# Splitting the logits of every second attention step around half a value tile

## The chip, the cores and the metric

The kernel runs on one core of one Trainium2 chip. The core has five engines with an instruction queue each: TensorE (matmuls, called PE in the profile), VectorE (DVE), ScalarE (ACT), GpSimd (POOL) and SyncE (SP, which here only issues DMAs). Each queue is worked through in order, and the engines wait for one another on semaphores. The metric is the time of one execution on the device in microseconds (us): before the change 1191.71 us, the median of 5 runs from 1191.21 to 1194.92.

## The reference, cut to what matters

Four layers run one after the other on a residual stream x of 2048 positions by 576 features: attention, gated MLP, attention, gated MLP.

```python
x = x + _A_ref(_layernorm(x), A_wqkv, A_wo)
x = x + _B_ref(_layernorm(x), B_w_in, B_w_sp, B_b_sp, B_w_out)
x = x + _A_ref(_layernorm(x), A_wqkv, A_wo)
x = x + _B_ref(_layernorm(x), B_w_in, B_w_sp, B_b_sp, B_w_out)
```

The attention has 32 heads of 18 features. Position s attends to 8 positions, s, s-2, ..., s-14, those below 0 masked:

```python
idx = pos[:, None] - off[None, :]          # off = 0, 2, ..., 14
logits = einsum('bhsd,bhswd->bhsw', q, kg) * scale
attn = softmax(where(mask, logits, -1e9))
o = einsum('bhsw,bhswd->bhsd', attn, vg)   # then o @ wo
```

The MLP multiplies gelu(x @ w_in[:, :half]) by a gate, which mixes the normalized other half over all positions with a 2048 by 2048 matrix, and projects back with w_out.

## The kernel before, in words

An attention layer (`layer_A`) cuts the 2048 queries into 19 tiles of 112 (the last has 32), each with its 16 preceding keys, so that a tile's keys are 128 rows. The window is not gathered: q and k carry extra rows that make the logit of every key outside the window very small, so full 128 by 112 logit blocks can be computed and exponentiated. 

Each tile is worked in two steps of 16 heads, 38 steps `s` in all (`NST`). A step uses these pieces, named as in the code:

- `L_mm(s)` (line 428): 16 matmuls of 32 by 128 weights and 112 columns into two PSUM tiles `L_ps`, `jp` = 0 and 1, 8 matmuls each. Heads lie in groups of 32 rows, and a matmul uses only the 32-row strip `32*j` of the array (`tile_position`). Half `jp` = 0 uses strips 0 and 1, half `jp` = 1 strips 2 and 3. Both tiles come from the tag `H`, which has two slots, so each half of step s+1 writes the slot that the same half of step s used, and waits until that has been read.
- `EXP(s)` (line 442): two ScalarE activations, one for each half, from `L_ps` to `P_sb` in SBUF. There are four `P_sb` buffers, two steps' worth.
- `PV(s)` (line 449): 16 matmuls of the full array, 19 columns each (18 features and the row of ones that gives the softmax sum), into `O_ps`, then on VectorE a reciprocal and a product into `o_t`. After the second step of a tile, SP issues a transposing DMA from `o_t` to the ring buffer `oT`.
- `VW(t, hh, dve)` (line 375): half a v tile: 5 matmuls of the full array, 288 columns each, into a PSUM tile `pv`, then one cast to `v_ext`, on VectorE if `dve`, else on ScalarE. In the stretch of the change the half `hh` = 0 lies at even steps and is cast on VectorE, the half `hh` = 1 lies at odd steps and is cast on ScalarE.
- `WO(i, hh)` (line 487): half an output tile of 128 positions: 5 matmuls of 288 columns from `oT` into `pw`, then the residual sum on VectorE. `LN_STATS`, `LN_XN` (on GpSimd), `XST` and `LN_T` (a store and a transposing DMA on SP) follow for each tile.

`pv`, `O_ps`, `pw`, `pp` and `pt` share the PSUM tag `PT`, which has four slots handed out in program order.

All of this is in a manual schedule: each engine's queue holds its instructions in the order in which the Python code emits them. The loop at line 707 sets the order around the change. In step s it emits `L_mm(s + 1)`, `EXP(s + 1)`, `PV(s)`, and then what the dictionary `table` holds for s: the projections `PG` of the second half of q and k (up to step `PG_END` = 14), then `VW`, then the output pieces. So the logits run one step ahead of the product with v, and a v tile is made some steps before it is used: `VW(t, 0)` stands at step 2t-2, `VW(t, 1)` at 2t-1, and `PV` needs them at step 2t. The tile t = 9 of the first attention is an exception, made at steps 0 and 13, and in the first attention the v tiles up to 8 are made ahead of the loop.

From step 14 on, a usual step on TensorE is thus `L_mm(s + 1)`, `PV(s)`, one `VW` half, one `WO` half. Steps 22 and 23 of the first attention have no `WO`, nor have steps 21 and 22 of the second. Steps 25 and 32 of the first and 32 of the second have two.

Of the kernel before, what the change touches and what calls it, by code (L numbers as in the profile page):

```python
# [62 lines left out]
class K:  # L63
# [258 lines left out]
    def layer_A(self, li):  # L322
# [32 lines left out]
        def tdim(t):  # L355
            nq = min(QT, S - QT * t)
            return HALO + nq, nq
# [11 lines left out]
        def evac(out, in_, dve):  # L369
            if dve:  # L370
                nc.vector.tensor_copy(out=out, in_=in_)  # L371
            else:
                nc.scalar.copy(out=out, in_=in_)

        def VW(t, hh, dve):
            nk = tdim(t)[0]
            pv = self.PT_tile([P, 512], f32, "pv")
            for c in range(5):
                nc.tensor.matmul(pv[:nk, 0:288], lhsT=self.xnT[:, c, QT * t:QT * t + nk],  # L379
                                 rhs=wv_sb[:, c, hh * 288:(hh + 1) * 288], start=(c == 0), stop=(c == 4))  # L380
            evac(v_ext[:nk, t, 16 * hh:16 * hh + 16, 0:DH], pv[:nk, 0:288].rearrange("p (b d) -> p b d", d=DH), dve)
# [43 lines left out]
        NST = 2 * NT  # L425
        L_tiles = {}

        def L_mm(s):
            t, hf = divmod(s, 2)
            nk, nq = tdim(t)  # L430
            L_tiles[s] = [self.H_tile("L_ps") for _ in range(2)]
            for jp in range(2):
                for ftl in range(4):
                    g = 4 * hf + ftl
                    for jj in range(2):
                        j = 2 * jp + jj
                        nc.tensor.matmul(L_tiles[s][jp][:nk, jj, ftl * QT:ftl * QT + nq],  # L437
                                         lhsT=kT[32 * j:32 * j + 32, g, QT * t:QT * t + nk],
                                         rhs=qT[32 * j:32 * j + 32, g, QT * t + PADL:QT * t + PADL + nq],
                                         start=True, stop=True, tile_position=(32 * j, 0))  # L440

        def EXP(s):
            nk, nq = tdim(s // 2)
            for jp, L_ps in enumerate(L_tiles.pop(s)):
                Lv = L_ps[:, :, 0:4 * QT].rearrange("p a (b c) -> p a b c", c=QT)
                nc.scalar.activation(out=P_bufs[(2 * s + jp) % 4][:nk, :, :, 0:nq], in_=Lv[:nk, :, :, 0:nq], func=ACT.Exp,  # L446
                                     scale=scale)

        def PV(s):
            t, hf = divmod(s, 2)  # L450
            nk, nq = tdim(t)
            O_ps = self.PT_tile([P, 512], f32, "O_ps")
            for jp in range(2):
                for ftl in range(4):
                    for jj in range(2):
                        idx = 4 * ftl + 2 * jp + jj
                        nc.tensor.matmul(O_ps[:, idx * (DH + 1):(idx + 1) * (DH + 1)],  # L457
                                         lhsT=P_bufs[(2 * s + jp) % 4][:nk, jj, ftl, :],
                                         rhs=v_ext[:nk, t, 16 * hf + idx, :], start=True, stop=True)
            Ov = O_ps[:, 0:16 * (DH + 1)].rearrange("p (h e) -> p h e", e=DH + 1)  # L460
            o_t = o_bufs[t % len(o_bufs)]
            rec = sb.tile([P, 16], f32, name="rec", tag="rec", bufs=2)
            nc.vector.reciprocal(out=rec[:nq, :], in_=Ov[:nq, :, DH])
            nc.vector.tensor_tensor(out=o_t[:nq, 288 * hf:288 * (hf + 1)].rearrange("p (h d) -> p h d", d=DH),
                                    in0=Ov[:nq, :, 0:DH], in1=rec[:nq, :, None].to_broadcast([nq, 16, DH]), op=ALU.mult)
            if hf == 1:
                c0 = (QT * t) % (RING * P)
                if t < NT - 2:
                    nc.sync.dma_start_transpose(out=oT[:, :, c0:c0 + nq], in_=o_t[:nq, :])
# [191 lines left out]
        table = {}  # L661
# [5 lines left out]
        PG_END = 14  # L667
# [9 lines left out]
        for i in range(NS):  # L677
            t = -(-(i + 1) * P // QT) - 1
            s = 2 * t + (6 if li == 0 and t < 10 else 5 if t < NT - 5 else 4 if t < NT - 3 else 3)
# [17 lines left out]
        for k_, (d, qk, cc) in enumerate(pre):  # L697
            if k_ == (2 if li == 0 else 0):
                L_mm(0)
                EXP(0)  # L700
            PG(d, qk, cc, li > 0 or k_ < 4, q2)
            if li == 0 and k_ == 3:
                self.fill_window_rows(QK, 1)
# [1 line left out]
            VW(nvw - 1, 0, False)  # L705
            VW(nvw - 1, 1, False)
        for s in range(NST):
            if s + 1 < NST:
                L_mm(s + 1)
                EXP(s + 1)  # L710
            PV(s)
            for f, a in table.pop(s, []):
                f(*a)
# [339 lines left out]
```

The softmax here doesn't subtract the row's maximum and nothing guards it: scores larger than these inputs give would overflow.

## Time and profile before

| what | value |
|---|---|
| median of 5 runs | 1191.71 us (1191.21 to 1194.92) |
| the profiled execution's own time | 1191.21 us |
| its span, first to last instruction | 1189.4 us |
| TensorE clock granted | 0.998 |
| busy share of PE, DVE, ACT, POOL | 99%, 46%, 32%, 24% |
| first attention's steps (L_ps matmuls) | from 40 to 127 us of the span |
| second attention's steps | from 624 to 715 us |
| share of the chain that ended last: L_ps, O_ps, pv, pw | 2%, 3%, 3%, 3% |
| one exponential (128 by 896) | 0.92 us |
| one cast of pv on VectorE, on ScalarE | 0.45 us, 0.40 us |

The profile shows one execution. A busy TensorE is no proof that it does useful work at its full pace: the matmuls are pipelined, a matmul of 112 columns is shown with 0.21 us though the next may start 0.01 us later, and short waits hide under these bars. What counts for TensorE is therefore the distance from the start of one block of matmuls to the start of the next. In the timeline view a row gives the start, the time from the first start to the last end, the engine, the line, the operation, the tiles (out<-in), the shapes, the number of instructions that were merged, and in brackets the engine's idle time before the row and what ended it. The timelines of PE and ACT are read together: what TensorE waits for in a step is mostly the exponential of the step before.

### The profile page before, as it was taken

How to read it: one execution, taken by the hardware profiler on the slowest of the kernel's cores; microseconds unless marked ns; L12 is line 12 of the kernel's file. 1: busy time of each engine (PE TensorE's matmuls, PEld its weight loads, DVE VectorE, ACT ScalarE, POOL GpSimd, SP SyncE). 2: the span in 40 equal slices, each digit the busy share in tenths (PEclk: the TensorE clock that was granted, in tenths of full speed). 3: DMA queues.
4: the chain of work that ended last, by engine and by line, in shares of the span. 5: the costliest groups of instructions: out<-in, count | busy, mean ns of one | idle time of the engine just before them, and what ended most of it. 6: DMA issues, size and time to landing. Idle time of an engine off the chain costs nothing.

```text
span 1189.4 us, 20761 instructions
## 1 busy us (share of the span) xinstructions
PE 1179.4 (99%) x8554; PEld 619.7 (52%) x8554; DVE 547.1 (46%) x1206; ACT 376.6 (32%) x593; POOL 282.4 (24%) x383
## 2 busy tenths in 40 slices
PE   8999999999999999999999999999999999999998
PEld 5567544444444444457755774444444444444677
DVE  9688587323323323245556786753333233233321
ACT  6478677110110110202256786760110110111000
POOL 4668686000000000001153877530000000000000
PEclk9999999999999999999999999999999999999999
DMA  8999992000000000049646899800000000001332
GB/s 201 195 173 193 186 231 47 23 11 2 12 12 12 12 7 5 18 143 281 169 101 126 195 229 207 187 19 4 12 12 1 12 12 12 12 1 31 122 105 73
DMA packets 178103, 101.21 MB, mean 85 GB/s; under 512 B 134335, under 2 KB 159359, under 8 KB 178008
## 3 DMA queue, kind: packets, MB, share of 16 engines
q1 hardware_dynamic: 165144, 78.13, 30.0%
q0 software_dynamic: 6512, 16.00, 5.2%
q10 hardware_dynamic: 6352, 5.75, 1.6%
q8 instruction: 67, 1.10, 0.4%
q14 instruction: 28, 0.23, 0.1%
HBM read 42.39 MB, written 16.53 MB: 50 GB/s over the span
## 4 chain that ended last, share of the span: by engine, by line
PE 95%; DVE 1%; POOL 1%; DMA 1%; issue 1%; ACT 1%; SPq 0%; POOLq 0%; DVEq 0%; ACTq 0%
PE pg L887 42%; PE pz L869 12%; PE po L941 12%; PE pz L791 11%; PE pp L402 4%; PE pw L494 3%; PE pv L379 3%; PE O_ps L457 3%; PE L_ps L437 2%; PE pzs L791 1%; DMA QK<-win2a 1%; POOL QK L77 1%; ACT P_sb L446 1%; DVE ln_st L554 0%; POOL lnx_rstd L560 0%
## 5 line engine op out<-in xcount | busy, mean ns | idle before, releaser
L887 PE MATMUL pg<-Wq,Z 128*128 128x512 bf16 x2304 | 502.8, 379 | 0.0
L887 PEld LDWEIGHTS <-Z 128*128 128x128 bf16 x2304 | 225.0, 98 | 272.2
L891 DVE TENSOR_TENSOR g_tmp<-pg,ln_xn 128x512 f32<-128x512 f32 x144 | 99.6, 692 | 429.2 <-PE pg L887 429.2
L881 ACT ACTIVATE z1T<-pz 128x1024 bf16<-128x1024 f32 x72 | 73.7, 1024 | 513.8 <-PE pz L869 513.6
L77 POOL DMA_DIRECT2D wout<-in_B_w_out_dram x4 | 4.3, 1064 | 604.6 <-PE pg L887 604.6
L941 PE MATMUL po<-wout,Z 128*128 128x288 bf16 x1152 | 141.4, 286 | 0.0
L446 ACT ACTIVATE P_sb<-L_ps 128x896 bf16<-128x896 f32 (+1 forms) x152 | 126.7, 887 | 40.9 <-PE L_ps L437 40.3
L869 PE MATMUL pz<-xnT,w 128*128 128x512 bf16 (+1 forms) x640 | 136.0, 380 | 0.0
L941 PEld LDWEIGHTS <-Z 128*128 128x128 bf16 x1152 | 112.7, 98 | 28.8
L791 PEld LDWEIGHTS <-xnT 128*128 128x128 bf16 (+1 forms) x800 | 66.3, 97 | 80.9 <-issue 23.7
L791 PE MATMUL pz<-win2a,xnT 128*128 128x512 bf16 x384 | 104.8, 380 | 0.0
L892 DVE TENSOR_TENSOR Z<-g_tmp,z1T 128x512 bf16<-128x512 f32 x144 | 99.6, 692 | 9.7
L869 PEld LDWEIGHTS <-w 128*128 128x128 bf16 (+1 forms) x640 | 51.0, 97 | 80.1 <-issue 27.1
L402 PE MATMUL pp<-xnT,wqk_sb 128*128 128x512 bf16 x360 | 83.0, 380 | 0.0
L805 ACT ACTIVATE zp<-pz 128x1024 bf16<-128x1024 f32 x64 | 65.5, 1024 | 36.7 <-PE pz L791 32.7
L951 DVE TENSOR_TENSOR x_new<-po,xo 128x288 f32<-128x288 f32 (+1 forms) x64 | 28.8, 455 | 87.6 <-PE po L941 83.4
L791 PE MATMUL pz<-win2b,xnT 128*128 128x512 bf16 (+1 forms) x256 | 65.8, 380 | 0.0
L807 DVE CUSTOM_DVE_ANT_0 Z<-zp 128x1536 bf16<-128x1536 bf16 x32 | 56.3, 1759 | 13.4 <-ACT zp L805 13.3
L77 POOL DMA_DIRECT2D QK<-stg x81 | 50.6, 630 | 36.9 <-DVE stg L371 20.7
L379 PE MATMUL pv<-wv_sb,xnT 128*128 128x288 bf16 (+1 forms) x380 | 56.3, 287 | 0.0
L242 POOL TENSOR_SCALAR ln_xn<-x_new,ln_mv,ln_rstd 128x576 bf16<-128x576 f32 x23 | 52.7, 2293 | 2.0
L402 PEld LDWEIGHTS <-wqk_sb 128*128 128x128 bf16 x360 | 33.3, 98 | 36.2 <-issue 0.7
(114 smaller groups left out, 916.8 us busy)
## 6 DMA issues: line engine op xcount, KB each, us to landing
xres<-x_new SPq DMA_DIRECT2D x48, 288.0 KB
xo<-xres SPq DMA_DIRECT2D x32, 288.0 KB
wout<-in_B_w_out_dram POOLq DMA_DIRECT2D x4, 1296.0 KB, 8.9
xo<-xres SPq DMA_DIRECT2D x8, 576.0 KB
w<-in_B_w_in_dram SPq DMA_DIRECT2D x16, 256.0 KB
QK<-stg POOLq DMA_DIRECT2D x53, 72.0 KB, 4.6
QK<-stg SPq DMA_DIRECT2D x41, 72.0 KB
xo<-in_A_x_dram SPq DMA_DIRECT2D x8, 288.0 KB
```

What stands on the lines that cost most here:

```text
L77: return eng.dma_start(out=out, in_=in_)
L379: nc.tensor.matmul(pv[:nk, 0:288], lhsT=self.xnT[:, c, QT * t:QT * t + nk], rhs=wv_sb[:, c, hh * 288:(hh + 1) * 288], start=(c == 0), stop ...
L402: nc.tensor.matmul(pp[:, :], lhsT=w, rhs=self.xnT[:, c, PADL + cc * 512:PADL + (cc + 1) * 512], start=(c == 0), stop=(c == 4))
L446: nc.scalar.activation(out=P_bufs[(2 * s + jp) % 4][:nk, :, :, 0:nq], in_=Lv[:nk, :, :, 0:nq], func=ACT.Exp, scale=scale)
L791: nc.tensor.matmul(pzvs[ci][:, sub * 512:sub * 512 + w], lhsT=self.xnT[r0:r1, c, PADL + i * P:PADL + (i + 1) * P], rhs=win2(c)[r0:r1, c0 + ...
L805: nc.scalar.activation(out=zp[:, c0:c0 + cn], in_=pzvs[ci][:, 0:cn], func=ACT.Gelu_apprx_tanh, accum_out=sums[:, ci:ci + 1])
L869: nc.tensor.matmul(pz1s[q // 2][:, q % 2, :], lhsT=w1[r0:r1, c, sub * P:(sub + 1) * P], rhs=self.xnT[r0:r1, c, PADL + q * 512:PADL + (q + ...
L881: nc.scalar.activation(out=z1T[:, q2 * 512:(q2 + 2) * 512], in_=pz1s[q2 // 2][:, :, :].rearrange("p a b -> p (a b)"), func=ACT.Gelu_apprx_ ...
L887: nc.tensor.matmul(pg[:, :], lhsT=Z[:, jj, i, sub * P:(sub + 1) * P], rhs=Wq[q][:, i, :], start=(i == 0), stop=(i == NS - 1))
L891: nc.vector.tensor_tensor(out=tmp[:], in0=pg[:, :], in1=bsp[:, qs], op=ALU.add)
L892: nc.vector.tensor_tensor(out=uT(jj)[:, sub, qs], in0=tmp[:], in1=z1Ts[jj, sub][:, qs], op=ALU.mult)
L941: nc.tensor.matmul(acc[hh], lhsT=uT(j // 2)[:, j % 2, i * P:(i + 1) * P], rhs=wouts[j // NJH][:, j % NJH, hh * 288:(hh + 1) * 288], start= ...
```

## The change

`L_mm` and `EXP` take the halves that they are to do (`jps`). In the loop, an even step from `PG_END` on that has a `VW(t, 0)`, with s + 1 below 36, emits logits half 0 of step s+1 and its exponential, then `VW(t, 0)`, then logits half 1 and its exponential, and then `PV(s)` and the rest of the table. That holds at steps 18, 20, ..., 34 of the first attention (9 steps) and 14, 16, ..., 34 of the second (11 steps). Number and kind of the instructions stay as they were. On TensorE the five matmuls of `VW` stand ahead of 8 logit matmuls and the 16 of `PV`; on VectorE the cast of `pv` stands ahead of the reciprocal and the product of `PV(s)`; the order on ScalarE, GpSimd and SP is unchanged. The `PT` slots are handed out in the order `pv`, `O_ps`, `pw` instead of `O_ps`, `pv`, `pw` in these steps.

```diff
-        def L_mm(s):
+        def L_mm(s, jps=(0, 1)):
             t, hf = divmod(s, 2)
             nk, nq = tdim(t)
-            L_tiles[s] = [self.H_tile("L_ps") for _ in range(2)]
-            for jp in range(2):
+            if 0 in jps:
+                L_tiles[s] = [self.H_tile("L_ps") for _ in range(2)]
+            for jp in jps:
                 for ftl in range(4):
...
-        def EXP(s):
+        def EXP(s, jps=(0, 1)):
             nk, nq = tdim(s // 2)
-            for jp, L_ps in enumerate(L_tiles.pop(s)):
+            for jp in jps:
+                L_ps = L_tiles[s][jp]
...
         for s in range(NST):
-            if s + 1 < NST:
+            vws = [e for e in table.get(s, []) if e[0] is VW]
+            if s >= PG_END and s + 1 < NST - 2 and vws and vws[0][1][1] == 0:
+                L_mm(s + 1, (0,))
+                EXP(s + 1, (0,))
+                VW(*vws[0][1])
+                table[s].remove(vws[0])
+                L_mm(s + 1, (1,))
+                EXP(s + 1, (1,))
+            elif s + 1 < NST:
                 L_mm(s + 1)
                 EXP(s + 1)
             PV(s)
```

## The prediction

> **What bounds the kernel now.** I read the page first. It says that TensorE is busy for 99% of the span, and that the chain of work that ended last is 95% TensorE; nothing off TensorE counts unless it makes TensorE wait.
>
> ```profile
> span 1189.4 us, 20761 instructions
> ...
> PE 1179.4 (99%) x8554; PEld 619.7 (52%) x8554; DVE 547.1 (46%) x1206; ACT 376.6 (32%) x593; POOL 282.4 (24%) x383
> ...
> PE 95%; DVE 1%; POOL 1%; DMA 1%; issue 1%; ACT 1%; SPq 0%; POOLq 0%; DVEq 0%; ACTq 0%
> ```
>
> Then the timeline of TensorE over two and a half steady steps of the second attention (first an odd step, 27, then the even step 28, then 29).
>
> ```profile
> 694.37 0.55 PE L437 MATMUL L_ps<-QK 32*128 32x112 bf16 x16
> 694.85 0.56 PE L457 MATMUL O_ps<-v_ext,P_sb 128*128 128x19 bf16 x16
> 695.26 0.77 PE L379 MATMUL pv<-wv_sb,xnT 128*128 128x288 bf16 x5
> 695.87 0.78 PE L494 MATMUL pw<-wo_sb,oT 128*128 128x288 bf16 x5
> 696.58 0.40 PE L437 MATMUL L_ps<-QK 32*128 32x112 bf16 x16
> 696.92 0.56 PE L457 MATMUL O_ps<-v_ext,P_sb 128*128 128x19 bf16 x16
> 697.33 0.77 PE L379 MATMUL pv<-wv_sb,xnT 128*128 128x288 bf16 x5
> 697.94 0.78 PE L494 MATMUL pw<-wo_sb,oT 128*128 128x288 bf16 x5
> 698.65 0.55 PE L437 MATMUL L_ps<-QK 32*128 32x112 bf16 x16
> ```
>
> From start to start, the logits take 0.48 us in the odd step and 0.34 in the even one (0.33 where exact), PV 0.41, VW 0.61, WO 0.71. An even step is 2.07 us, an odd one 2.21. There is no bubble; the only loss is the 0.15 us by which the odd step's logits are longer. ScalarE's timeline over the same time says why:
>
> ```profile
> 692.77 1.73 ACT L446 ACTIVATE P_sb<-L_ps 128x896 bf16<-128x896 f32 x2 [0.20 <-PE L_ps L437]
> 694.84 1.73 ACT L446 ACTIVATE P_sb<-L_ps 128x896 bf16<-128x896 f32 x2 [0.34 <-PE L_ps L437]
> 696.45 0.41 ACT L373 CAST v_ext<-pv 128x288 bf16<-128x288 f32 x1
> ```
>
> The second exponential begun in the even step ends at 694.50, 0.13 us after the next logits began; their second half has to wait for it. In the even step it is over (694.84 + 1.73 = 696.57, logits at 696.58) and nothing waits. Exponentials start 0.47 us after the logits' first matmul (694.84 - 694.37, 697.05 - 696.58) and follow each other at 0.86 or 0.87.
>
> What half a logit block costs alone is to be seen where ScalarE is the limit, at step 21, which has no WO:
>
> ```profile
> 683.32 0.37 PE L437 MATMUL L_ps<-QK 32*128 32x112 bf16 x8
> 684.05 0.37 PE L437 MATMUL L_ps<-QK 32*128 32x112 bf16 x8 [0.36 <-ACT P_sb L446]
> 684.36 0.56 PE L457 MATMUL O_ps<-v_ext,P_sb 128*128 128x19 bf16 x16
> 684.77 0.77 PE L379 MATMUL pv<-wv_sb,xnT 128*128 128x288 bf16 x5
> 685.48 0.87 PE L437 MATMUL L_ps<-QK 32*128 32x112 bf16 x16
> ```
>
> Eight matmuls take 0.37 where sixteen take 0.40: a half uses two row strips instead of four, so its matmuls queue on the same strip. From 684.05 to PV at 684.36 a half takes 0.30 to 0.31. And VW followed by logits takes 0.71 (684.77 to 685.48), followed by WO 0.61: going over from full-array matmuls to strips costs 0.10.
>
> **The change part by part.** *Split logits.* An even step now holds half 0, VW, half 1, PV, WO: 0.30 + 0.71 + 0.30 + 0.42 + 0.71 = 2.44 us, against 0.33 + 0.42 + 0.61 + 0.71 = 2.07 where nothing waits: **+0.37** (0.30 + 0.30 - 0.33 for the halves, 0.10 for the second entry into strips). Below, it could be 0.22: 0.15 less if both halves ran at the whole block's pace, 0.08 less each. I take 0.37, the row of a half alone.
>
> The drain rule speaks against this change. The row first: the five starts of a 288-column block lie 0.12 apart (0.61 / 5), but 0.22 pass from the last VW matmul to the first logit (0.71 - 4 x 0.12), and 0.14 from the last logit to PV (694.37 + 0.55 - 0.21 = 694.71, PV at 694.85). The Trainium skill, "TensorEngine Tiling (Array Packing)", section Key Properties, says that changing the tiling mode, not merely the tile, drains TensorE. With the warm latency of "TensorE: Matmul & The Clock Gate", section Single matmul latency, (398 + N) / 2.4 ns, a full drain would be an estimated 0.29 us after VW and 0.21 after logits, where rows show 0.22 and 0.14. By the pages a split would then cost 0.14 more, some 2.8 us over 20 steps; I keep the rows.
>
> *Waits that go.* In the new even step, with its start at 0, half 1 starts at 1.01 and its exponential at 1.48 instead of 1.33; it ends at 2.40 (0.92 alone). The odd step's logits start at 2.44: both halves are free, so the odd step's 0.15 goes, with 0.04 to spare. Even steps that waited themselves gain too, since half 1 comes 1.01 us later. ScalarE works 4 x 0.87 + 0.41 = 3.9 us in a pair of now 4.5.
>
> *VW's cast* goes ahead of the reciprocal on VectorE. It is ready at about 1.15 in the step, PV's product only at about 1.9, so nothing queues behind it for long; in a pair VectorE has some 3.7 us of work (18.86 busy in the 22 us from 690 to 712, by the table of windows), cover enough. If that went, o_t would be late by at most one cast, 0.45, ahead of a transpose that is needed two to four steps on. PV is later in the even step by about 1 us; its probabilities are read by 1.9, a microsecond before the exponential of the next step writes those buffers again. The PSUM slot that VW now takes is that of a WO two steps back, summed by VectorE a step ago. No DMA is moved, and nothing on SP's or POOL's queue changes place.
>
> *Summed by pairs.* I read each pair's two logit blocks from the timeline and take what lies over 0.33 as removable.
> Second attention: pairs from 14, 16, 18, 20 (0.49/0.33, 0.49/0.37, 0.45/0.39, 0.42/0.39) give +0.21, +0.17, +0.19, +0.22; from 24 to 30 (0.33 or 0.34, then 0.48) four times +0.22. Pair 22 (1.04/0.80) is limited by ScalarE; between 0 and 0.37 I take 0.20. Pair 32 has no wait (0.33/0.33): +0.37. At step 34 the v tile is 48 rows wide and already has a change of mode around it, and its logits waited (0.49): +0.03. Sum 2.3 us.
> First attention: 18, 20 (0.46/0.39, 0.43/0.39) +0.18, +0.21; 22 (0.43/1.00) and 24 (0.50/0.33) +0.20 each; 26, 28, 30 (0.33/0.49) +0.21 each; 32 +0.37; 34 +0.03. Sum 1.8 us.
>
> *What the first attention gives back.* Behind its last steps TensorE stands idle:
>
> ```profile
> 128.50 0.61 PE L791 MATMUL pz<-win2a,xnT 128*128 128x512 bf16 x2
> 130.14 0.41 PE L494 MATMUL pw<-wo_sb,oT 128*128 128x288 bf16 x2 [1.03 <-DVE o_t L464]
> ```
>
> From start to start that is 1.64 where two such matmuls and a change take 0.44, so 1.2 us are spare. The view names a VectorE product. The pw slot was free long before; I take the releaser to be the last oT transpose, issued by SP at 125.56 and landed at 130.00 by the trace's landing times. By its timeline SP issues without a pause from 104.74 on, when its wait for the residual buffer of step 25 ended. Step 25 comes 0.8 us later by the sums above, so the transpose lands about 0.8 later, and TensorE, arriving 1.8 later, finds it there: the first attention costs +0.8, not +1.8. If the queue caught up wholly, 0.6 is the least (1.8 - 1.2); if VectorE is the releaser, all 1.8 stay. The second attention has no such idle time (716.05 to 716.49).
>
> Sum: 2.3 + 0.8 = **+3.1 us**. The profiled execution took 1191.21 us, 0.5 below the median: 1194.3 for it, **1194.8** as a median.
>
> **The rivals.**
> *A, the forecast:* +3.1; its own range, from the pair sums' rounding and the give-back, 1194.2 to 1195.6.
> *B, dearer:* the later second exponential becomes a wait of the odd step. The spare is 0.04; if it is 0.1 short, 14 odd steps pay 0.1, +1.4. Or no give-back, +1.0. Together 1195.8 to 1197.2. For it: the margin is thin, and the releaser is read against the view. Against it: every term of the margin is a row.
> *C, cheaper:* the halves run at the whole block's pace (0.22 a split): 2.7 less over 18 full splits, of which the first attention can give back only to 0; +0.4 to +2.2, 1192.1 to 1193.9. Against it: the x8 rows of 0.37.
> *D, faster:* the waits removed are worth 7.0 (18 x 0.37 + 2 x 0.19) - 4.1 = 2.9 us. If a split cost nothing, 1188.8. It decides only where a split costs under 0.02 us (2.9 - 2.4 over 20), that is if TensorE could start half 1 without the second entry and with all four strips at work. The 0.71 against 0.61 speaks against it.
>
> **How the numbers follow.** A 0.50, B 0.19, C 0.27, D 0.04. About 0.2%, 2.4 us, is what a measurement of this kernel can tell from no change. A and B are beyond it on the slow side but for a part of A (0.02), C is within, D faster: slower 0.67, same 0.29, faster 0.04. The range leaves out D, the top of B and the bottom of C: 1192.6 to 1196.9; the likeliest case alone has 1194.2 to 1195.6.
>
> **What the profile after would show.** Right: in even steps two L_ps rows of 8 with 0.37 each and pv between them, pv to the second row 0.71, steps of 2.44; odd logits back at 0.33; pairs of 4.5 us instead of 4.28; the idle time at 130 us nearly gone; PE's span of the second attention 2.3 us longer. Wrong: x8 rows under 0.30, odd logits still at 0.48, the idle time at 130 still 1.2, or a new wait of pv for a PSUM slot.

## The result

The kernel takes 1194.79 us, the median of 32 runs (1192.36 to 1200.82), against 1191.21 for the kernel before (57 runs, 1188.79 to 1196.26). The ratio is 1.0029, with a 95% interval from 1.0021 to 1.0037, so the change costs 2.5 to 4.4 us. Forecast were 1194.8 us and a loss of 3.1. That the time agrees to 0.01 us is luck: the loss is 3.6 us, and the median of the kernel before is 0.5 us lower over 57 runs than over the 5 from which the forecast was counted.

### The profile page after: what moved, and what is told of

It is laid out like the page before. It is cut to its first block, busy times and chain, and to the rows that moved or that the text cites. A ratio compares the mean times of both kernels' runs of the same rounds, so it can differ in the third digit from the quotient of the medians.

```text
span 1196.3 us, 20771 instructions
## 1 busy us (share of the span) xinstructions
PE 1184.2 (99%) x8554; PEld 619.4 (52%) x8554; DVE 547.2 (46%) x1206; ACT 378.4 (32%) x593; POOL 279.8 (23%) x383
## 4 chain that ended last, share of the span: by engine, by line
PE 96%; DMA 2%; DVE 1%; ACT 0%; issue 0%; SPq 0%; POOL 0%; ACTq 0%; DVEq 0%
PE pg L897 42%; PE pz L879 12%; PE po L951 12%; PE pz L801 11%; PE pp L402 6%; PE pv L379 4%; PE pw L496 3%; PE O_ps L459 3%; PE L_ps L438 2%; PE pzs L801 1%; DMA oT<-o_t 1%; DMA xnT<-ln_xn 1%; ACT P_sb L448 0%; DVE ln_st L556 0%; DVE ln_xn L569 0%
## 5 line engine op out<-in xcount | busy, mean ns | idle before, releaser
L242 POOL TENSOR_SCALAR ln_xn<-x_new,ln_mv,ln_rstd 128x576 bf16<-128x576 f32 x23 | 52.7, 2293 | 2.0
```

## The profile after

The page of the changed kernel:

```profile
span 1196.3 us, 20771 instructions
...
PE 1184.2 (99%) x8554; PEld 619.4 (52%) x8554; DVE 547.2 (46%) x1206; ACT 378.4 (32%) x593; POOL 279.8 (23%) x383
...
PE 96%; DMA 2%; DVE 1%; ACT 0%; issue 0%; SPq 0%; POOL 0%; ACTq 0%; DVEq 0%
```

The span is 6.9 us longer than the one before, twice the change of the median. This execution took 1198.11 us, 3.3 above the median of its kernel, and 2.9 of the 6.9 us arose ahead of the first split of either attention. To see that, I measure TensorE's distances between the same points of the program in both traces:

| stretch on TensorE, us | before | after | difference |
|---|---|---|---|
| start to first logit of the first attention | 40.35 | 40.65 | +0.30 |
| from there to the logits of step 14 | 39.83 | 41.70 | +1.87 |
| step 14 to step 18 | 7.39 | 7.38 | 0 |
| **step 18 to step 35** (9 splits) | 37.19 | 39.13 | **+1.94** |
| step 35 to the output piece of tile 14 | 5.37 | 5.17 | -0.20 |
| first MLP, up to the second attention | as before | as before | 0 |
| first logit of the second attention to step 14 | 42.43 | 43.16 | +0.73 |
| **step 14 to step 35** (11 splits) | 45.59 | 47.82 | **+2.23** |
| from there to the end | as before | as before | 0 |

The sum is 6.87. The 1.87 and the 0.73 lie ahead of the first split; the list of waits on TensorE names DMAs there, the first of them once for 3.0 us (from 49.7 to 52.7 us):

```profile
PE pp L402 <- DMA xnT<-ln_xn: 3.0, 1, 3.0
PE L_ps L438 <- ACT P_sb L448: 2.0, 6, 0.4
PE warm L543 <- POOL ident L184: 1.5, 1, 1.5
PE pw L496 <- DMA oT<-o_t: 1.4, 2, 0.8
```

The first row is a wait of the projections for transposed rows. Of the two waits of `pw` for the oT DMA, one of 0.56 us stands ahead of step 14 of the second attention, the other, of 0.83 us, behind the last step of the first. The kernels below have the same code up to step 14 but for the two with late row transposes. The eight others need between 37.4 and 41.8 us from the first logit to step 14 in their profiles: this stretch varies from execution to execution, and it is the reason why spans of single executions can't be compared here.

The stretches with the splits vary less. That of the second attention takes 47.82 us in each of the three kernels that split it like this. In the first attention single steps are up to 1.3 us longer in some profiles (18 and 25), and step 16, ahead of the stretch, takes 2.8 to 4.3 us instead of 1.62 in three; where the list of waits names a cause, it is an output piece that waits for an oT transpose. TensorE's timeline of the changed kernel, step 26 of the second attention (even, split), step 27 and the beginning of 28:

```profile
698.09 0.37 PE L438 MATMUL L_ps<-QK 32*128 32x112 bf16 x8
698.39 0.79 PE L379 MATMUL pv<-wv_sb,xnT 128*128 128x288 bf16 x5
699.11 0.37 PE L438 MATMUL L_ps<-QK 32*128 32x112 bf16 x8
699.41 0.56 PE L459 MATMUL O_ps<-v_ext,P_sb 128*128 128x19 bf16 x16
699.82 0.77 PE L496 MATMUL pw<-wo_sb,oT 128*128 128x288 bf16 x5
700.53 0.40 PE L438 MATMUL L_ps<-QK 32*128 32x112 bf16 x16
700.86 0.56 PE L459 MATMUL O_ps<-v_ext,P_sb 128*128 128x19 bf16 x16
701.27 0.77 PE L379 MATMUL pv<-wv_sb,xnT 128*128 128x288 bf16 x5
701.88 0.78 PE L496 MATMUL pw<-wo_sb,oT 128*128 128x288 bf16 x5
702.59 0.37 PE L438 MATMUL L_ps<-QK 32*128 32x112 bf16 x8
```

From start to start: half 0.30, VW 0.72, half 0.30, PV 0.41, WO 0.71, together 2.44. The odd step's logits are back at 0.33 (700.53 to 700.86) and the step at 2.06. The pair is 4.50 us long; it was 4.28. ScalarE over the same time:

```profile
698.56 1.94 ACT L448 ACTIVATE P_sb<-L_ps 128x896 bf16<-128x896 f32 x2
701.00 1.73 ACT L448 ACTIVATE P_sb<-L_ps 128x896 bf16<-128x896 f32 x2 [0.51 <-PE L_ps L438]
```

The split step's two exponentials end at 698.56 + 1.94 = 700.50, 0.03 us ahead of the logits at 700.53. The margin on which the odd step's gain hung is as thin as forecast, and holds.

## The experiments

Two explanations were set against each other. By the first, a split has a **fixed cost** on TensorE (two halves alone instead of one block, one more entry into row strips), and only the odd step's wait comes back. By its rival, the loss is made by what comes **later**: the second exponential, PV behind VW, the cast ahead of the reciprocal, other PSUM slots. A second question was what the first attention gives back behind its last step. These are the stretches in each kernel's profile, in us; the third column is the idle time before the output piece of tile 14, its distance from step 35 less the 4.18 that it takes where nothing waits.

| kernel | first attention, 18 to 35 | idle before tile 14's piece | second attention, 14 to 35 | ratio to before |
|---|---|---|---|---|
| before | 37.19 | 1.19 | 45.59 | 1 |
| the change | 39.13 | 0.99 | 47.82 | 1.0029 (1.0021 to 1.0037) |
| second attention only | 37.78 | 1.09 | 47.82 | 1.0014 (1.0001 to 1.0028) |
| first attention only | 39.13 | 0 | 45.59 | 1.0008 (0.9994 to 1.0023) |
| short exponentials | 37.19 | 1.22 | 44.89 | 0.9993 (0.9979 to 1.0006) |
| short exponentials, split | 37.24 | 1.78 | 48.82 | 1.0017 (1.0003 to 1.0031) |
| split around PV | 38.87 | 0.94 | 47.73 | 1.0030 (1.0018 to 1.0041) |
| split at every step | 42.01 | 0 | 50.67 | 1.0064 (1.0045 to 1.0083) |
| late row transposes | 39.07 | 0 | 45.60 | 1.0096 (1.0073 to 1.0120) |
| late row transposes, split | 41.30 | 0 | 47.82 | 1.0109 (1.0093 to 1.0126) |

### The two attentions one at a time

```diff
-            if s >= PG_END and s + 1 < NST - 2 and vws and vws[0][1][1] == 0:
+            if li == 2 and s >= PG_END and s + 1 < NST - 2 and vws and vws[0][1][1] == 0:
```

> The split in the second attention alone (11 steps). Theory of the fixed cost (a split costs TensorE 0.37 us, 0.19 at step 34, and gives back only the waits for the exponential): from the first logit of step 14 to that of step 35 the second attention takes 47.8 us, as with the whole change, against 45.6 before; the kernel 2.2 us above before (ratio 1.0019). Rival, that the loss is mostly made by what the transposes and stores do in the first attention: under 1 us. The two parts add up to the whole (3.5 us) if they don't act on each other.

With `li == 0` in its place:

> The split in the first attention alone (9 steps). Fixed cost: from the first logit of step 18 to that of step 35 the first attention takes 39.1 us against 37.2 before, and a part comes back in the idle time before the output piece of tile 14. My prediction had 1.0 of 1.8 come back, so +0.8; the profile of the whole change shows only 0.2 to 0.4 come back, so +1.4 to +1.7 (ratio 1.0012 to 1.0014). The second attention, steps 14 to 35, stays at 45.6.

Each stretch has the length that it has with the whole change, and the other attention that of the kernel before (the 0.6 more in the first attention's stretch of the first kernel is all in step 18, which has no split there: 2.83 us instead of 2.19, with an output piece that waits 0.46 for an oT transpose, and that step is 2.19 to 2.21 in the other unsplit ones with on-time transposes). The times, +1.7 (0.1 to 3.3) and +1.0 us (-0.7 to 2.7), fit the expectations of 2.2 and 1.4 to 1.7, and are too wide to say more. In the second profile the idle time behind the first attention is gone. Its timeline of TensorE:

```profile
129.49 0.60 PE L801 MATMUL pz<-win2a,xnT 128*128 128x512 bf16 x2
129.93 1.39 PE L496 MATMUL pw<-wo_sb,oT 128*128 128x288 bf16 x10
```

From the two matmuls to the output piece it is 0.44 us, the bare time, where the kernel before had 1.64: here the whole 1.2 came back, and the first attention lost 43.31 - 42.56 = 0.75 us from step 18 to that piece. In the profile of the whole change, whose first attention has the same code, 0.2 came back.

### The price of a split with ScalarE out of the way

```diff
-                nc.scalar.activation(out=P_bufs[(2 * s + jp) % 4][:nk, :, :, 0:nq], in_=Lv[:nk, :, :, 0:nq], func=ACT.Exp,
+                nf = 2 if li == 2 and s > PG_END else 4
+                nc.scalar.activation(out=P_bufs[(2 * s + jp) % 4][:nk, :, 0:nf, 0:nq], in_=Lv[:nk, :, 0:nf, 0:nq], func=ACT.Exp,
                                      scale=scale)
```

> Before, but in the second attention the exponentials that are issued from step 14 on do only 2 of their 4 column groups (the other heads' probabilities are left as they were two steps before, so half of the softmax weights are stale there): ScalarE then never keeps TensorE waiting. Fixed cost theory: all logit blocks of steps 14 to 35 fall to 0.33 us, steps 14 to 35 take 45.6 - 2.6 = 43.0 us, the kernel is 2.6 us faster than before. It measures what waits there are to win at most.

The same with the split in the second attention:

> The same short exponentials, with the split in the second attention alone. Nothing waits for ScalarE in either, so the difference to the kernel with short exponentials alone is the bare price of 11 splits. Fixed cost: 10 x 0.37 + 0.19 = 3.9 us, steps 14 to 35 take 46.9 us, the kernel 1.3 us above before. Rival, that the change loses time because half 1 and with it the exponential and PV come later: with ScalarE far from busy that costs nothing, steps 14 to 35 stay at 43.0 and the kernel stays 2.6 us under before.

Both kernels leave out half of the exponentials of those steps and so compute another result than the attention's; they only serve to measure. Step by step the expectation holds: without the split all logit blocks from step 15 on fall to 0.33 us (0.35 at step 22) and a pair to 4.12; with it, the split steps take 2.44 instead of 2.06. But the stretch did not shrink by 2.6. In the kernel with short exponentials, TensorE's timeline has this at step 25:

```profile
693.06 0.79 PE L495 MATMUL pw<-wo_sb,oT 128*128 128x288 bf16 x5 [1.62 <-DMA oT<-o_t]
```

And the timeline of the one with the split has this at step 32:

```profile
712.13 0.79 PE L497 MATMUL pw<-wo_sb,oT 128*128 128x288 bf16 x5 [1.19 <-DMA oT<-o_t]
```

An output piece waits for a transposing DMA of oT that was hidden before. From start to start step 25 is 3.86 instead of 2.06 us, +1.79; with the split, step 32 is 1.36 longer and step 25 0.33. Without these waits the two stretches are 44.89 - 1.79 = 43.10 and 48.82 - 1.36 - 0.33 = 47.13. The first is the 43.0 that was expected; the difference is 4.03 where 3.9 was expected for 11 splits, 0.24 of it a wait for the exponential that is left at step 23. So a split costs 0.38 us (2.44 against 2.06) with no exponential to wait for, and the rival, which had this at nothing, is out. What had not been expected is that of 2.5 us won on ScalarE's waits 1.8 went back to a DMA.

### Another block between the halves

```diff
                 L_mm(s + 1, (0,))
                 EXP(s + 1, (0,))
-                VW(*vws[0][1])
-                table[s].remove(vws[0])
+                PV(s)
                 L_mm(s + 1, (1,))
                 EXP(s + 1, (1,))
...
                 L_mm(s + 1)
                 EXP(s + 1)
-            PV(s)
+                PV(s)
+            else:
+                PV(s)
```

> The same 20 steps split, but PV(s) instead of VW stands between the halves: half 0, PV, half 1, VW, WO. Half 1 then starts 0.8 us into the step instead of 1.0, its exponential is not later than before, the cast and PV keep their order on VectorE and the PSUM slots theirs. Fixed cost: 0.30 + 0.50 + 0.30 + 0.61 + 0.71 = 2.42 us a split step, +3.0 to +3.7 us on the kernel, about as with VW. Rival (late exponential, late PV, the order of cast and reciprocal, or another PSUM slot makes the loss): the loss shrinks to under 1 us.

TensorE's timeline of the beginning of one split step:

```profile
701.58 0.37 PE L438 MATMUL L_ps<-QK 32*128 32x112 bf16 x8
701.88 0.56 PE L459 MATMUL O_ps<-v_ext,P_sb 128*128 128x19 bf16 x16
702.38 0.37 PE L438 MATMUL L_ps<-QK 32*128 32x112 bf16 x8
702.68 0.54 PE L379 MATMUL pv<-wv_sb,xnT 128*128 128x288 bf16 x3
```

Half 0.30, PV 0.50, half 0.30: the split step takes 2.43 us, the ratio is 1.0030. With the cast, PV, the slots and the exponential in their old places the loss is the same. What they have in common with the change is the split itself.

### Twice as many splits

```diff
-            if s >= PG_END and s + 1 < NST - 2 and vws and vws[0][1][1] == 0:
+            if s >= PG_END and s + 1 < NST - 2 and vws:
```

> The split in every step from 14 on that has a VW, the odd ones too (their cast, on ScalarE, then stands between the two exponentials). Fixed cost: 10 more splits in the second and 8 more in the first attention at 0.37 each with no wait left to win, but for steps 21 to 23 of the two, where ScalarE is the limit: steps 14 to 35 of the second attention 47.8 + 3.3 to 3.7 = 51.1 to 51.5 us, 18 to 35 of the first 39.1 + 2.6 to 3.0 = 41.7 to 42.1, the kernel 8.5 to 10.5 us above before. Rival (a split is nearly free where nothing waits for the exponential): under 5 us above before.

The second attention takes 50.67 us: 2.85 more than the change, a little under the 3.3 expected at least. Eight odd steps go to 2.44, +0.35 to 0.38 each, and step 21 has 0.36 more, while the steps that ScalarE limits, 22 and 23, are 0.09 and 0.41 shorter. The first attention takes 42.01 (42.1 expected at most), 0.5 of it in step 18 as above. The kernel is 7.6 us above before (5.4 to 9.9), below the expected 8.5 to 10.5 in the middle, though the interval reaches into it. In its profile step 16 of the first attention, which has no split, takes 4.09 us instead of 1.62, with an output piece that waits 2.3 for an oT transpose; this lies outside the stretches of the table. In the odd steps, which had already been relieved of their waits, a split gives back nothing but at the steps that ScalarE limits.

### What waits behind the first attention

```diff
-                at(max(s + 4, 24 + (5 * i) // 4) if li == 0 else s + 4, LN_T, i)
+                at(max(s + 4, 38 + i if i >= 4 else 0) if li == 0 else s + 4, LN_T, i)
```

> Before, with the transposes of the normalized rows of tiles 4 to 14 (LN_T) of the first attention put behind its last step, so that SP and the DMA queue have the oT transposes of the last steps sooner. If the last oT transpose is what the output piece of tile 14 waits for, its 1.2 us of idle time in front go, and the kernel is 1.0 to 1.2 us faster than before, if nothing in the MLP waits for the later rows. If VectorE is what it waits for, the idle time stays and nothing changes.

The same with the change:

> The change, with the same late LN_T of the first attention. If the oT transpose is the releaser, no part of the loss can come back at the end of the first attention: 1.9 + 2.2 = 4.1 us above the kernel with late LN_T alone, 2.9 to 3.1 above before. If the releaser is VectorE: as the change without it, 3.5 above before.

The edit also puts the transposes of tiles 0 to 3 earlier (steps 12 to 18 instead of 24 to 27), which the expectation does not say; the steps of the first attention that are longer without a split, 18 and 25, may come from that, but step 18 is longer in two kernels without this edit too. The idle time before tile 14's piece is gone in both, as expected if the oT transpose in the DMA queue released it. But both kernels are 11 and 13 us slower than before: the stretch of the first MLP from the last output piece to the first gate matmul took 87.3 and 86.4 us instead of 77.4. ScalarE's timeline of the first of them shows where:

```profile
148.62 0.20 ACT L805 ACTIVATION_READ_ACCUMULATOR zp<-pz 128x1 f32 x1
157.19 0.84 ACT L809 ACTIVATE Z<-zp 128x768 bf16<-128x768 bf16 x1 [8.37 <-DMA xnT<-stg]
```

The MLP's `Z` waits until the late transposes have read the normalized rows in `stg`; most likely the two share SBUF, since one is allocated after the other has been given back. My condition "if nothing in the MLP waits for the later rows" failed: it is not the rows that are needed, but the place where they lie. So the idle time went when the oT transposes were freed, which fits the oT transpose as its releaser, and the edit is no way to win the 1.2 us. Between the two the stretches differ by 2.2 and 2.2 us, the medians by 2.4 where 4.1 was expected; the first MLP, 0.9 shorter in the one with the split, hides part of it, and with six runs each (1200.5 to 1209.3 and 1204.5 to 1206.9) the 2.4 is rough. Moving these transposes by a few steps only was not measured, and the kernel before and the change have one profile each.

## Why the prediction was right, and where it was not

- **Split logits, +0.37:** measured +0.38 (2.444 against 2.063, the unsplit step without a wait). Its pieces are 0.30 for a half, twice, and 0.72 for VW with an entry into strips behind it. They were read off rows of step 22 of the kernel before (not 21, as the prediction has it: step 21 ends at 683.32 us, where the rows begin), where ScalarE's limit had already separated the halves; that a row elsewhere in the same trace shows the new situation is what made the number good to 0.01 us.
- **Waits that go:** the odd step's 0.15 went in every pair that had it, with a margin of 0.03 (0.04 forecast). The prediction puts exponentials 0.86 or 0.87 apart; from its own rows it is 0.81 (1.73 for two, 0.92 for one), which the margin does not use. Rival B's first half, a new wait in the odd steps, did not come: what is left at step 17, 0.03, was 0.04 before. Only step 23, where ScalarE is the limit, waits 0.31 longer than before, and step 22 is 0.25 shorter for it.
- **VW's cast, PV and the PSUM slots at nothing:** no wait of pv for a slot appears in the changed kernel's list of waits, and the kernel with the split around PV, which leaves them where they were, loses as much.
- **Second attention, +2.3:** +2.23. Pair 22, which ScalarE limits, was put at 0.20 and cost 0.07 (4.76 against 4.69 us).
- **First attention, +1.8:** +1.94 up to step 35.
- **What it gives back, 1.0:** the one mis-sized term, and it is no fixed number. The releaser was named rightly against the view of the kernel before: the list of waits after says itself that `pw` waits for the oT DMA. By the trace's landing times the output piece starts 0.14 us behind the transpose in both kernels (landed at 130.00 and 133.90, started at 130.14 and 134.03), while in the changed kernel VectorE's last product ends at 134.10, when the piece has begun. The queue of the kernel before, and then queue and TensorE of the changed one:

```profile
125.56 1.19 SPq L469 DMA_TRANSPOSE oT<-o_t  x1
```

```profile
128.90 1.19 SPq L471 DMA_TRANSPOSE oT<-o_t  x1
```

```profile
134.03 0.65 PE L496 MATMUL pw<-wo_sb,oT 128*128 128x288 bf16 x4 [0.83 <-DMA oT<-o_t]
```

The step that was off is "so the transpose lands about 0.8 later". The queue did start again 0.85 later, counted from step 18. But the transpose was issued 1.2 later and took 5.0 us to land instead of 4.4, so it landed 1.74 later in the profile of the change. With the split in the first attention alone it landed 0.74 later, as forecast, and the whole 1.2 came back. In the profiles with the split in the first attention the idle time is 0.99, 0, 0.94 and 0 us (0 with late transposes too), in those without it 1.09 to 1.78: between 0.2 and all of it comes back. Since the same code gave 0.99 and 0, this is a difference between executions; what sets it in the DMA queue stays open.
- **Rivals:** C, halves at the pace of the whole block, is refuted by the rows of 8 with 0.37. D needed a split under 0.02 us. The drain rule of the Trainium skill, "TensorEngine Tiling (Array Packing)", Key Properties, points the right way: changing over costs time here, 0.72 from VW to logits against 0.61 from VW to WO. By the prediction's estimate from the latency formula of "TensorE: Matmul & The Clock Gate", Single matmul latency, full drains would have given 0.51 a split; the 0.38 that was measured is what the rows had said. C's range of +0.4 to +2.2 does not follow from its own terms, 0.15 less for 10 and for 8 splits: they leave 0.8 in the second attention and 0 to 0.6 in the first, so +0.8 to +1.4. As C did not come, nothing hangs on it.

By the stretches of the profiled execution the change costs 1.94 - 0.20 + 2.23 = 4.0 us, by the medians 3.6, with an interval from 2.5 to 4.4. The forecast of 3.1 lies inside it; the difference of 0.5 is less than the 1.0 by which the idle time behind the first attention differs between profiles of the same code.

## What to carry to other kernels

When matmuls that use parts of the array are grouped in a block, breaking the block up has two prices, the overlap between its parts and another entry and exit, and they are to be set against the very wait that the break removes: here, in a usual pair of steps, 0.38 paid for 0.15. A wait of the busiest engine on another engine is worth only as much as the next wait behind it allows; look for the rows, often at an irregular step, that already show the block broken up. And where starts vary by microseconds from run to run, compare distances between fixed points of the program, not spans.

## What had not been expected of the hardware

- Sixteen logit matmuls in one block start within 0.195 us, eight on two strips within 0.16. In the whole block of the kernel before at 696.58 us, the matmul that carries the second half's semaphore wait starts 0.03 us after the block's first, ahead of most of the first half's: so the strips work side by side across the halves, and a split gives that up.
- The stretch before step 14 of the first attention, with the same instructions in eight kernels, took from 37.4 to 41.8 us in single profiles. The list of waits names DMAs for the long ones. This is larger than the change under study.
- With its exponentials shortened, the second attention lost 1.8 us to a wait for an oT transpose, which the kernel before did not show in that stretch.
